# One written order of issue in place of a planner, with fewer spare matmuls, in the first part of a fused attention and Fourier-FFN kernel

## The chip, the cores and the metric

The kernel runs on one core of one Trainium2 chip. The metric is device microseconds of one execution: 995.22 us for the kernel before, the median of 3 runs (994.12 to 995.35).

## The reference, cut to what matters

```python
def _attn_ref(q, k, v, g_norm):            # 8 batches, 8 heads, 576 tokens, head size 64
    kv = np.einsum('bhsd,bhse->bhde', k, v)
    out = np.einsum('bhsd,bhde->bhse', q, kv)
    rms = np.sqrt(np.mean(out * out, axis=-1, keepdims=True) + 1e-06)
    return out / rms * g_norm

def _moe_ref(x, w_ch1, w_ch2):             # x: 8 x 576 x 512; w_ch1: 512 x 2048; w_ch2: 2048 x 512
    X = np.fft.fft(np.fft.fft(x, axis=1), axis=2)
    u = x + np.real(X)
    mu = np.mean(u, axis=-1, keepdims=True)
    var = np.mean((u - mu) ** 2, axis=-1, keepdims=True)
    un = (u - mu) / np.sqrt(var + 1e-06)
    return u + np.maximum(un @ w_ch1, 0.0) @ w_ch2
```

The two weights come as float64 and are decoded on the chip from their bits.

## The kernel before, in words

**What is computed where.** The work has a first part and a late part. The first part takes the eight batches one after the other, with their steps interleaved. For each batch `plan_kv` multiplies keys and values (TensorE, L1197), `plan_q` turns the queries (L1273 for batches 0 and 1, L1279 for the others) and ScalarE copies the turned tile out (`take`, L1283). `plan_out` forms the attention output of three groups of rows t = 0, 1, 2 (L1304); batch 0 has its own form, `plan_first_out` (L1374), with squares (ScalarE L1388), sums (VectorE L1391), a refined reciprocal root (L1403 to L1411) and a scaling (L1419). `plan_fold` folds the rows for the transform: a fold on VectorE (L1501), two sums "even" (L1508, on GpSimd for batch 0), a rounded high part on ScalarE (L1514) and the low remainder (L1517, GpSimd). `plan_seq` is the transform along the tokens (TensorE L1544 for batch 0, L1532 after it; low part on VectorE, L1569), `plan_chn` the one along the channels (L1586; VectorE L1608 and L1628), `plan_turn` the transpose of the result into blocks of 512 tokens (TensorE L1684, high part ScalarE L1693, low part VectorE L1696). Every matmul of weight is done three times, on high and low parts.

As soon as a block of 512 tokens is turned, `plan_early` runs three slices of the FFN on it: `plan_first` (TensorE L1012) and the second product (L1029). Block 0 lies wholly in batch 0. So the first L1012 matmul, step number 1528 below, needs the whole chain of batch 0: keys and values, first output, fold, seq, chn, turn. `plan_w` loads and decodes a weight slice: a load (SyncE, L1729 with the copy at L936), ScalarE L939, VectorE L946 to L956 and L1743, for the first weight a mean on TensorE (L970) and its subtraction (L979), then high (ScalarE L1763) and low (L1768, on GpSimd for the first weight's early slices). The late part, from about 360 us, is the rest of the FFN.

**Spare matmuls.** `plan_spare` (L1075) makes 200 steps of two matmuls that write to a PSUM bank and are read by nobody:

```python
def go(ps=ps):
    for _ in range(0 if pools else 2):
        nc.tensor.matmul(ps.t, still, wide, start=True, stop=True)
```

A step that is issued once the late part's memory is opened (`close`, L2023) emits nothing.

**What sets the order.** Every step is an `Op` with an engine, a cost, a rank, the steps that it needs, and the buffers that it uses, which come from rings of a fixed number of slots (for instance two tiles of queries, six of keys and values, eight PSUM banks). Each engine issues its steps in the order in which they are emitted and waits at the first whose inputs are missing. Before, `Plan.go` (L638) finds that order by playing the steps through with the costs, the ranks and a table `MOVES` of corrections to ranks; it puts spare steps where it has nothing else for TensorE. `Plan.settle` (L796) then applies a table `SHIFTS`: single steps moved on their engine by some places, or left out. `Plan.emit` (L819) emits.

Of the kernel before, what the change touches and what calls it, by code (L numbers as in the profile page):

```python
# [76 lines left out]
SHIFTS = [  # L77
    ("plan_spare.go/PE/-/-", 20, 0),
    ("plan_w.<lambda>/DVE/w1/2", 3, -1),
    ("plan_w.<lambda>/DVE/w1/1", 1, -2),  # L80
    ("plan_q.take/ACT/3/11", 0, 2),
    ("plan_spare.go/PE/-/-", 18, 0),
    ("plan_spare.go/PE/-/-", 26, 0),
    ("plan_w.<lambda>/DVE/w2/2", 1, -4),
    ("plan_first_out.mean/DVE/0/1", 0, -2),
    ("plan_chn.<lambda>/DVE/1/1", 1, -6),
    ("plan_spare.go/PE/-/-", 31, 0),
    ("plan_first_out.square/ACT/0/2", 1, 9),
    ("plan_chn.<lambda>/ACT/1/2", 0, 5),
    ("plan_fold.even.go/DVE/1/1", 1, -2),  # L90
    ("plan_fold.fold/DVE/1/0", 0, -6),
    ("plan_spare.go/PE/-/-", 16, 0),
    ("plan_kv.<lambda>/POOL/2/-", 1, 9),
    ("plan_kv.<lambda>/POOL/5/-", 1, -2),
    ("plan_seq.<lambda>/PE/0/1", 0, -1),
    ("plan_turn.high/ACT/0/0", 0, -2),
    ("plan_out.red/DVE/2/1", 1, 10),
    ("plan_seq.<lambda>/PE/0/0", 1, 2),
    ("plan_q_load.load/SP/1/02", 0, 10),
    ("plan_spare.go/PE/-/-", 9, -4),  # L100
    ("plan_fold.mul/DVE/2/0", 0, -4),
    ("plan_q_load.<lambda>/SP/3/-", 0, 1),
    ("plan_spare.go/PE/-/-", 27, 0),
    ("plan_out.<lambda>/ACT/2/1", 0, -1),
    ("plan_kv.<lambda>/DVE/0/-", 0, 9),
    ("plan_fold.zero/ACT/1/1", 0, 4),
    ("plan_out.<lambda>/ACT/2/1", 1, 1),
    ("plan_first.<lambda>/PE/e0/-", 9, 3),
    ("plan_chn.put.<lambda>/SP/0/0", 1, 2),
    ("plan_kv.<lambda>/SP/1/-", 8, 1),  # L110
    ("plan_fold.zero/ACT/2/2", 0, -1),
    ("plan_chn.mix/DVE/0/0", 1, 5),
    ("plan_y.last/DVE/2/-", 0, -1),
    ("plan_seq.<lambda>/PE/0/0", 0, -2),
    ("plan_out.<lambda>/ACT/1/0", 1, 4),
    ("plan_kv.go/PE/1/-", 1, 1),
    ("plan_w.<lambda>/ACT/w2/0", 0, 9),
    ("plan_first.<lambda>/PE/e0/-", 4, 1),
    ("plan_first_out.mean/DVE/0/2", 0, 1),
    ("plan_first_out.mul/DVE/0/1", 0, 1),  # L120
    ("plan_early.<lambda>/ACT/e0/-", 3, -4),
    ("plan_out.scale/POOL/1/2", 0, 8),
    ("plan_chn.<lambda>/DVE/0/0", 0, 1),
    ("plan_kv.<lambda>/SP/5/-", 8, -2),
    ("plan_q.turn/PE/2/12", 0, 1),
    ("plan_fold.fold/DVE/0/2", 0, -2),
    ("plan_kv.<lambda>/POOL/2/-", 0, 9),
    ("plan_spare.go/PE/-/-", 28, 0),
    ("plan_chn.mix/DVE/1/1", 0, -1),
    ("plan_kv.<lambda>/SP/5/-", 3, 4),  # L130
    ("plan_seq.mm/PE/1/3", 0, -2),
    ("plan_turn.high/ACT/0/0", 1, -2),
    ("plan_out.<lambda>/ACT/2/1", 0, 1),
    ("plan_fold.even.go/POOL/2/0", 1, 3),
    ("plan_fold.low/POOL/1/2", 0, -2),
    ("plan_q.take/ACT/2/11", 0, 7),
    ("plan_early.<lambda>/PE/e0/-", 10, -1),
    ("plan_out.scale/POOL/2/1", 1, 1),
    ("plan_spare.go/PE/-/-", 22, 0),
    ("plan_first_out.red/DVE/0/2", 1, -6),  # L140
    ("plan_fold.zero/ACT/1/2", 0, -2),
    ("plan_q.take/ACT/3/11", 0, -9),
    ("plan_w.<lambda>/DVE/w2/1", 1, 6),
    ("plan_first_out.red/DVE/0/2", 0, 1),
    ("plan_w.<lambda>/DVE/w2/0", 0, 9),
    ("plan_kv.<lambda>/SP/5/-", 7, 7),
    ("plan_w.<lambda>/DVE/w2/1", 0, 8),
    ("plan_first.<lambda>/DVE/e0/-", 1, -1),
    ("plan_spare.go/PE/-/-", 34, 0),
    ("plan_spare.go/PE/-/-", 33, 1),  # L150
    ("plan_chn.<lambda>/ACT/0/1", 0, 3),
    ("plan_q.turn/PE/4/01", 0, 9),
    ("plan_turn.turn/PE/0/1", 0, -2),
    ("plan_q.take/ACT/0/01", 0, -7),
    ("plan_chn.mm/PE/1/0", 1, 4),
    ("plan_turn.high/ACT/0/2", 1, -2),
    ("plan_chn.put.<lambda>/SP/0/0", 1, -2),
    ("plan_q_load.load/SP/1/-", 0, -1),
    ("plan_y.root/ACT/1/-", 0, 3),
    ("plan_w.<lambda>/DVE/w2/1", 5, -6),  # L160
    ("plan_spare.go/PE/-/-", 19, 0),
    ("plan_turn.low/DVE/0/1", 2, -1),
    ("plan_first.<lambda>/PE/e0/-", 0, -2),
    ("plan_turn.high/ACT/4/0", 2, 4),
    ("plan_out.red/DVE/2/1", 1, -3),
    ("plan_kv.<lambda>/POOL/3/-", 0, 1),
    ("plan_kv.<lambda>/ACT/6/-", 0, -2),
    ("plan_q.turn/PE/7/02", 0, 1),
    ("plan_chn.add_r/POOL/5/1", 0, -1),
    ("plan_early.<lambda>/ACT/e1/-", 7, 1),  # L170
    ("plan_y.recip/DVE/4/-", 0, -2),
    ("plan_early.<lambda>/ACT/e2/-", 5, -3),
    ("plan_fold.<lambda>/ACT/2/0", 0, -4),
    ("plan_turn.low/DVE/1/2", 0, 3),
    ("plan_out.red/DVE/6/2", 0, 1),
    ("plan_q.take/ACT/7/10", 0, 1),
    ("plan_first.<lambda>/PE/e2/-", 3, -1),
    ("plan_kv.<lambda>/SP/3/-", 9, -3),
    ("plan_out.mm/PE/3/2", 0, 6),
    ("plan_out.scale/POOL/4/2", 0, -3),  # L180
    ("plan_fold.<lambda>/ACT/3/1", 0, 9),
    ("plan_out.mm/PE/4/0", 0, 1),
    ("plan_chn.<lambda>/DVE/2/2", 1, 2),
    ("plan_chn.<lambda>/DVE/4/0", 0, 4),
    ("plan_first.<lambda>/PE/e3/-", 11, -6),
    ("plan_early.<lambda>/PE/e1/-", 7, -1),
    ("plan_early.<lambda>/ACT/e3/-", 3, -3),
    ("plan_out.og/ACT/6/1", 0, -7),
    ("plan_q.take/ACT/4/11", 0, -10),
    ("plan_turn.turn/PE/1/1", 0, 2),  # L190
    ("plan_seq.mm/PE/3/3", 0, 3),
    ("plan_chn.add_l/POOL/5/1", 0, 1),
    ("plan_seq.low/DVE/3/1", 0, -1),
    ("plan_q_load.load/SP/3/-", 0, 4),
    ("plan_kv.<lambda>/SP/4/-", 4, 2),
    ("plan_early.<lambda>/ACT/e1/-", 3, 1),
    ("plan_chn.<lambda>/DVE/0/0", 1, 9),
    ("plan_seq.mm/PE/3/0", 0, 2),
    ("plan_seq.mm/PE/3/2", 0, 3),
    ("plan_fold.<lambda>/ACT/3/1", 0, 4),  # L200
    ("plan_first.<lambda>/ACT/e3/-", 1, -1),
    ("plan_fold.low/DVE/1/1", 0, -1),
    ("plan_seq.<lambda>/ACT/2/1", 0, -2),
    ("plan_q.take/ACT/2/11", 0, -3),
    ("plan_turn.high/ACT/2/0", 3, 2),
    ("plan_turn.high/ACT/3/0", 3, 1),
    ("plan_chn.add_r/POOL/5/1", 0, -1),
    ("plan_out.<lambda>/ACT/6/0", 0, -2),
    ("plan_fold.<lambda>/ACT/1/1", 0, -4),
    ("plan_fold.low/DVE/2/2", 0, -2),  # L210
    ("plan_turn.low/DVE/1/1", 2, -1),
    ("plan_chn.<lambda>/DVE/3/2", 0, -3),
    ("plan_first.<lambda>/ACT/e2/-", 2, -2),
    ("plan_y.last/DVE/2/-", 0, -3),
    ("plan_kv.<lambda>/POOL/4/-", 1, 3),
    ("plan_seq.mm/PE/5/0", 0, 1),
    ("plan_turn.low/DVE/3/2", 0, -1),
    ("plan_out.og/ACT/5/2", 1, 3),
    ("plan_fold.<lambda>/ACT/1/1", 0, -2),
    ("plan_first.<lambda>/ACT/e2/-", 0, -1),  # L220
    ("plan_chn.mm/PE/5/2", 1, 2),
    ("plan_chn.mm/PE/5/2", 0, -4),
    ("plan_kv.go/PE/5/-", 1, -1),
    ("plan_turn.low/DVE/1/2", 2, -1),
    ("plan_turn.turn/PE/1/0", 1, 1),
    ("plan_chn.<lambda>/DVE/2/1", 0, 4),
    ("plan_fold.even.go/POOL/4/1", 1, -4),
    ("plan_fold.even.go/POOL/2/1", 1, -6),
    ("plan_fold.<lambda>/ACT/3/1", 0, -1),
    ("plan_out.red/DVE/4/1", 0, 6),  # L230
    ("plan_chn.mm/PE/3/0", 1, 9),
    ("plan_kv.<lambda>/POOL/4/-", 1, -2),
    ("plan_first.<lambda>/PE/e2/-", 1, -2),
    ("plan_kv.<lambda>/SP/6/-", 4, 1),
    ("plan_turn.low/DVE/2/0", 2, 9),
    ("plan_q.turn/PE/7/10", 0, 9),
    ("plan_fold.low/POOL/4/1", 0, 1),
    ("plan_fold.low/DVE/4/2", 0, -2),
    ("plan_first.<lambda>/ACT/e1/-", 2, 2),
    ("plan_out.mm/PE/6/2", 0, 2),  # L240
    ("plan_early.<lambda>/ACT/e1/-", 5, 2),
    ("plan_turn.low/DVE/3/1", 1, 2),
    ("plan_chn.put.<lambda>/SP/3/2", 2, 4),
    ("plan_y.mean/POOL/4/-", 0, 2),
    ("plan_first.<lambda>/ACT/e0/-", 0, -3),
    ("plan_chn.<lambda>/ACT/2/1", 0, -1),
    ("plan_turn.high/ACT/0/0", 2, -2),
    ("plan_fold.mul/DVE/3/2", 1, -2),
    ("plan_out.og/ACT/4/2", 1, 1),
    ("plan_seq.low/DVE/5/1", 0, -1),  # L250
    ("plan_kv.<lambda>/POOL/7/-", 1, 1),
    ("plan_turn.high/ACT/4/0", 2, 1),
    ("plan_first.<lambda>/PE/e1/-", 4, -1),
# [2271 lines left out]
```

## Time and profile before

| | |
|---|---|
| median of the runs | 995.22 us (994.12 to 995.35) |
| span of the profiled execution, first to last instruction | 993.5 us |
| TensorE busy | 982.3 us (99%), 6838 matmuls |
| VectorE busy | 690.1 us (69%) |
| ScalarE busy | 363.4 us (37%) |
| GpSimd busy | 397.6 us (40%) |
| DMA | 166.06 MB, mean 167 GB/s |

The page gives the span of the profiled execution and no other time of it; the median of the runs is 1.7 us above it. A busy TensorE is one that has a matmul in flight: matmuls are pipelined, so one of 512 columns shows about 0.39 us, while the next starts about 0.23 us after it. In the windows below, PEclk is the granted clock as a share of 2.4 GHz; 0.5 is 1.2 GHz.

### The profile page before, as it was taken

How to read it: one execution, taken by the hardware profiler on the slowest of the kernel's cores; microseconds unless marked ns; L12 is line 12 of the kernel's file. 1: busy time of each engine (PE TensorE's matmuls, PEld its weight loads, DVE VectorE, ACT ScalarE, POOL GpSimd, SP SyncE). 2: the span in 40 equal slices, each digit the busy share in tenths (PEclk: the TensorE clock that was granted, in tenths of full speed). 3: DMA queues.
4: the chain of work that ended last, by engine and by line, in shares of the span. 5: the costliest groups of instructions: out<-in, count | busy, mean ns of one | idle time of the engine just before them, and what ended most of it. 6: DMA issues, size and time to landing. Idle time of an engine off the chain costs nothing.

```text
span 993.5 us, 17707 instructions
## 1 busy us (share of the span) xinstructions
PE 982.3 (99%) x6838; PEld 858.5 (86%) x6838; DVE 690.1 (69%) x1365; ACT 363.4 (37%) x731; POOL 397.6 (40%) x391
## 2 busy tenths in 40 slices
...
GB/s 231 236 222 271 210 275 230 200 161 165 144 195 117 267 168 192 181 252 211 225 170 159 201 44 212 44 212 53 202 81 187 100 171 115 153 107 149 1 127 43
DMA packets 111240, 166.06 MB, mean 167 GB/s; under 512 B 43710, under 2 KB 71666, under 8 KB 104756
## 3 DMA queue, kind: packets, MB, share of 16 engines
...
q8 instruction: 54, 0.88, 0.4%
...
## 4 chain that ended last, share of the span: by engine, by line
PE 94%; DMA 3%; SPq 1%; DVE 1%; issue 0%; ACT 0%; DVEq 0%; ACTq 0%
PE acc L1029 40%; PE ps_h L1012 20%; PE ps_h L2251 18%; PE ps_f L1586 4%; PE ps_f L1532 3%; PE ps_o L1304 3%; PE ps_k L1197 2%; PE ps_t L1684 2%; DMA vm<-in_v_dram 1%; PE ps_q L1279 1%; DMA draw<-in_dft_s_dram 1%; DMA qt<-in_q_dram 1%; PE ps_s L1084 1%; PE ps_o L1374 0%; SPq L1174 0%
## 5 line engine op out<-in xcount | busy, mean ns | idle before, releaser
L1029 PE MATMUL acc<-w,hh 128*128 128x512 f32 x1150 | 359.3, 394 | 0.0
L1029 PEld LDWEIGHTS acc<-w,hh 128*128 128x128 f32 x1150 | 205.7, 189 | 34.2
L1029 PE MATMUL acc<-w,hl 128*128 128x512 f32 x575 | 224.0, 390 | 0.0
L1021 ACT ACTIVATE hh<-ps_h 128x512 fp32r<-128x512 f32 x144 | 86.2, 598 | 345.8 <-DVE ps_h L2259 170.9
L1012 PE MATMUL ps_h<-unTh,w 128*128 128x512 f32 x576 | 179.3, 392 | 0.0
L1024 DVE SCALAR_TENSOR_TENSOR hl<-ps_h,hh 128x512 fp32r<-128x512 f32 x144 | 98.0, 684 | 92.1 <-ACT hh L1021 91.8
L1029 PEld LDWEIGHTS acc<-w,hl 128*128 128x128 f32 x575 | 108.0, 188 | 23.6
L1012 PEld LDWEIGHTS ps_h<-unTh,w 128*128 128x128 f32 x576 | 106.6, 188 | 21.3
L1012 PE MATMUL ps_h<-unTl,w 128*128 128x512 f32 x288 | 112.3, 390 | 0.0
L2211 POOL TENSOR_TENSOR up<-up 128x512 f32<-128x512 f32 x36 | 46.6, 1295 | 154.4 <-DMA up<-next_scr 119.2
L2259 DVE TENSOR_TENSOR ps_h<-part,ps_h 128x256 f32<-128x256 f32 x144 | 61.1, 425 | 40.9 <-ACT part L2264 23.3
L2259 DVE TENSOR_TENSOR part<-part,ps_h 128x256 f32<-128x256 f32 x108 | 45.4, 420 | 44.4 <-PE ps_h L2251 41.5
L1012 PEld LDWEIGHTS ps_h<-unTl,w 128*128 128x128 f32 x288 | 54.1, 188 | 11.5
L2224 POOL TENSOR_TENSOR uu<-uu,up 128x512 f32<-128x512 f32 x36 | 46.9, 1312 | 36.9 <-ACT up L2216 36.9
L1353 POOL TENSOR_TENSOR x<-x,gb 96x512 f32<-96x512 f32 (+1 forms) x26 | 33.8, 1311 | 45.0 <-ACT x L1320 45.0
L2264 ACT COPY part<-ps_h 128x256 f32<-128x256 f32 x36 | 13.4, 373 | 81.4 <-PE ps_h L2251 81.4
L1696 DVE TENSOR_TENSOR unTl<-ps_t,unTh 128x384 fp32r<-128x384 f32 (+13 forms) x80 | 34.0, 477 | 9.0 <-ACT unTh L1693 8.9
L2358 DVE SCALAR_TENSOR_TENSOR uu<-acc,bz,uu 128x512 f32<-128x512 f32 x35 | 25.0, 750 | 20.2 <-PE acc L1029 20.2
L1508 POOL TENSOR_TENSOR xe<-ab 96x256 f32<-96x256 f32 (+1 forms) x32 | 25.0, 797 | 34.0 <-DVE ab L1501 32.7
L1340 DVE TENSOR_REDUCE ss<-ps_o 96x8 f32<-96x512 f32 (+1 forms) x42 | 27.9, 682 | 14.1 <-ACT ps_o L1336 13.9
L1586 PE MATMUL ps_f<-cd,pt 128*96 128x258 f32 (+1 forms) x288 | 37.0, 283 | 0.0
L1586 PEld LDWEIGHTS ps_f<-cd,pt 128*96 128x96 f32 (+1 forms) x288 | 35.0, 162 | 1.3 <-DVE ss L1340 0.2
(226 smaller groups left out, 1875.9 us busy)
## 6 DMA issues: line engine op xcount, KB each, us to landing
...
```

Of the source, the lines that this page charges most:

```text
L1012: nc.tensor.matmul(ps, w[c][:, kc * P : (kc + 1) * P], unT[a][:, kc, :], start=(kc == 0 and n == 0), stop=(kc == KC - 1 and n == 2),)
L1021: nc.scalar.activation(hh, ps, AF.Relu)
L1024: nc.vector.scalar_tensor_tensor(hl, ps, 0.0, hh.bitcast(F32), ALU.max, ALU.subtract)
L1029: nc.tensor.matmul(acc, hpair[a][:, i * P : (i + 1) * P], w[c], start=(first and n == 0), stop=(last and n == 2),)
L1304: nc.tensor.matmul(pss[s].t[:n, at : at + D], fqs[side].t[half, m, :n], kvt.t[half, m], start=True, stop=True,)
L1353: nc.gpsimd.tensor_tensor(v_, v_, gb[:n].unsqueeze(1).to_broadcast([n, H, D]), ALU.mult)
L1586: nc.tensor.matmul(ps.t[:n, :ND], pt.t[a][:, part, ch, offs[t] : offs[t] + n], cd[:, part, c, ch, :], start=(idx == 0), stop=(idx == 5),)
L1696: nc.vector.tensor_tensor(unTs[j].t[1][:, :, to], view()[:, :, lo:hi], unTs[j].t[0][:, :, to].bitcast(F32), ALU.subtract,)
L2211: lambda p=part: nc.gpsimd.tensor_tensor(p.t[:, 0], p.t[:, 0], p.t[:, 1], ALU.add),
L2224: lambda k=k, ut=ut, p=part: nc.gpsimd.tensor_tensor(ut.t[:, k], ut.t[:, k], p.t[:, 0], ALU.add),
L2251: nc.tensor.matmul(x(to), w.t[:, c, i, kk * P : (kk + 1) * P], rhs(a, kk), start=(kk == 0 and n == 0), stop=(kk == 1 and n == 2),)
L2259: return op("DVE", 415, URGENT, lambda: nc.vector.tensor_tensor(out(), a(), b(), ALU.add), d, bufs)
```

## The change

`SHIFTS`, `MOVES`, `Plan.go`, `Plan.settle` and the planner's constants go. A table `ORDER` has the numbers of 4137 steps in the order of emission; `run` emits it, after testing that no step stands ahead of one that it needs. No step, its work, its engine or its buffers are changed; only places, and the spare steps.

```diff
-SHIFTS = [
-    ("plan_spare.go/PE/-/-", 20, 0),
-    ("plan_w.<lambda>/DVE/w1/2", 3, -1),
...
-MOVES = {
-    "<lambda>/HOST/0/12": 30,
-    "<lambda>/POOL/2": -0.5,
...
+ORDER = """
+5 242 209 381 234 219 210 215 227 226 216 207 206 4 235 42 8 382 383 384 385 386 387 388 213 2 212 218 393 211
+208 222 221 39 389 228 232 237 230 48 23 217 57 214 220 53 239 223 390 391 233 229 392 241 447 238 231 236 394
+240 224 403 452 467 395 396 397 398 0 399 400 225 243 254 401 404 247 245 402 405 406 407 246 408 248 265 244
+256 249 267 269 258 474 454 451 462 466 276 453 277 450 459 460 281 280 449 457 257 250 251 268 259 252 253 270
+261 290 271 260 255 470 266 293 292 482 448 262 263 264 296 272 273 409 410 275 274 294 278 471 298 299 295 461
+468 475 61 472 463 456 415 411 455 464 458 302 279 412 304 305 476 291 469 300 473 282 465 413 306 600 601 414
+301 307 416 283 417 418 419 284 609 287 607 603 606 602 610 604 627 1 612 313 497 477 479 318 319 323 324 314
+325 315 498 501 502 499 480 478 288 285 316 326 503 420 421 500 286 422 327 317 505 481 289 490 308 309 310 320
+483 611 423 311 321 620 613 425 615 616 605 619 491 494 312 322 424 328 329 346 484 487 492 495 485 488 330 348
+493 496 331 486 332 347 362 363 614 628 617 608 364 426 297 629 303 349 489 350 365 427 352 351 366 428 368 367
+334 333 635 504 755 756 338 341 26 357 354 623 625 339 342 344 618 360 624 626 621 371 622 374 358 372 355 506
+429 343 345 430 431 340 432 375 373 356 508 652 376 630 433 379 631 762 763 758 757 760 759 773 761 764 656 657
+377 653 654 434 658 380 361 655 378 643 765 1528 632 1534 1535 1536 1537 1529 1530 1531 507 509 510 511 520 527
...
     def run(self):
...
+        seen = set()
+        line = [self.ops[int(n)] for n in ORDER.split()]
+        for o in line:
+            seen.add(o.n)
+            if any(a.n not in seen for a in o.after):
+                raise RuntimeError(f"{o.key} stands ahead of what it needs")
+        self.emit(line)
```

What stands at some numbers, with the step's place on its own engine in the two orders (counted from 0, spare steps included on TensorE):

| number, step | engine | before | after |
|---|---|---|---|
| 393, load of slice 0 of the second weight | SyncE | 1 | 13 |
| 221 and 222, last keys and values of batch 0 | SyncE | 16, 17 | 17, 16 |
| 239, last turn of queries of batch 0 | TensorE | 14 | 16 |
| 223, last keys-times-values of batch 0 | TensorE | 25 | 17 |
| 394, first step on weight slice 393; 240, copy of 239's result; 224, copy of the keys-times-values | ScalarE | 8, 4, 9 | 7, 8, 9 |
| 243, first output, t = 2 | TensorE | 28 | 18 |
| 470, a turn of queries of batch 1 | TensorE | 38 | 23 |
| 266, first output, t = 0, second product | TensorE | 33 | 24 |
| 302, fold of batch 0, t = 0 | VectorE | 40 | 43 |
| 408, 409, 410, decoding of slice 1 of the first weight | VectorE | 41, 42, 43 | 19, 39, 40 |
| 304 and 305, "even" of batch 0, t = 0 | GpSimd | 15, 16 | 12, 13 |
| 414, low part of slice 1 of the first weight | GpSimd | 14 | 16 |
| 301 and 307, low parts of batch 0, t = 1 and t = 0 | GpSimd | 13, 18 | 17, 18 |
| first and last seq step of batch 0 | TensorE | 46, 62 | 34, 49 |
| 322, seq low part, last of the four | VectorE | 62 | 61 |
| 427 to 430, decoding of slice 2 of the first weight | VectorE | 59, 61, 63, 64 | 74, 78, 81, 84 |
| 328, first chn step of batch 0 | TensorE | 69 | 52 |
| 623, 625, 621, turns of queries of batch 2 | TensorE | 78, 80, 77 | 67, 68, 69 |
| 765, first keys-times-values of batch 3 | TensorE | 89 | 76 |
| 361, the last low part of block 0's turn | VectorE | 97 | 95 |
| 1528, first FFN step of block 0 | TensorE | 93 | 77 |
| 632, a turn of queries of batch 2 | TensorE | 90 | 78 |

Spare steps that emit matmuls: before, 27 on TensorE's places 0 to 8, 13, 19 to 21, 23, 24, 26, 27, 35, 36, 41, 42, 50, 56, 81, 94, 95 and 329; after, 9 on places 1 to 3, 9, 10, 12, 15, 28 and 64.

## Rows read from the trace of the kernel before

**Rows 1.** Windows: stretch, its us, busy us (instructions) by engine, PEclk, DMA, GB/s

```profile
46.70:62.30 15.60, 15.19 (x252) 13.85 (x250) 12.78 (x23) 7.46 (x17) 6.49 (x9) 1.00 0.95 259
62.30:78.80 16.50, 16.41 (x220) 14.63 (x218) 15.62 (x39) 11.99 (x29) 7.22 (x10) 1.00 0.76 201
78.80:360.00 281.20, 281.20 (x2342) 246.83 (x2340) 210.06 (x414) 147.94 (x334) 121.25 (x152) 1.00 0.64 202
360.00:993.50 633.50, 628.54 (x3486) 548.94 (x3484) 422.75 (x835) 178.35 (x316) 252.29 (x201) 1.00 0.41 144
```

**Rows 2.** Windows of the spare matmuls alone: us, PE busy, PEld busy, PEclk, DMA, GB/s

```profile
0.00:9.40 9.40, 7.05 (x18) 5.22 (x18) 1.00 0.73 217
9.40:24.40 15.00, 4.72 (x16) 2.69 (x16) 1.00 1.04 241
34.50:41.30 6.80, 2.07 (x4) 1.16 (x4) 0.52 1.17 202
41.30:78.80 37.50, 3.19 (x10) 1.63 (x10) 1.00 0.87 226
78.80:360.00 281.20, 1.71 (x6) 1.13 (x6) 1.00 0.64 202
```

**Rows 3.** Timeline of TensorE: start, us, instructions merged, idle time before them and its releaser

```profile
9.34 0.88 PE L1273 MATMUL ps_q<-ident,qt 96*64 96x96 f32 x16 [0.59 <-DMA qt<-in_q_dram]
...
13.71 2.20 PE L1273 MATMUL ps_q<-ident,qt 96*64 96x96 f32 x48 [0.26 <-DMA qt<-in_q_dram]
...
24.40 1.57 PE L1374 MATMUL ps_o<-kvt,fq 64*96 64x64 f32 x32
...
33.35 0.81 PE L1374 MATMUL ps_o<-kvg,fq 64*97 64x64 f32 x13 [1.17 <-ACT fq L1283]
...
46.75 0.51 PE L1544 MATMUL ps_f<-cs,xh 96*128 96x290 f32 x2
...
49.69 0.51 PE L1197 MATMUL ps_k<-vm,km 128*64 128x64 f32 x10 [0.20 <-DMA vm<-in_v_dram]
...
78.81 0.73 PE L1012 MATMUL ps_h<-unTh,w 128*128 128x512 f32 x2
...
92.36 0.73 PE L1029 MATMUL acc<-w,hh 128*128 128x512 f32 x2
...
93.85 0.62 PE L1029 MATMUL acc<-w,hh 128*128 128x512 f32 x2
94.31 0.39 PE L1029 MATMUL acc<-w,hl 128*128 128x512 f32 x1
```

**Rows 4.** Timeline of ScalarE, the two loads that it waited for

```profile
24.62 0.64 ACT L939 ACTIVATE ps_a<-raw 128x512 f32<-128x512 f32 x1 [0.86 <-DMA raw<-in_moe_w_ch_dram]
...
32.00 0.93 ACT L1113 ACTIVATE cs<-draw 97x870 fp32r<-97x870 f32 x1 [2.20 <-DMA draw<-in_dft_s_dram]
```

**Rows 5.** Timeline of VectorE, batch 0's chain

```profile
27.23 1.27 DVE L1391 TENSOR_REDUCE ss<-ps_o 96x8 f32<-96x512 f32 x2
...
41.53 0.68 DVE L1501 TENSOR_TENSOR part<-x 97x512 f32<-97x512 f32 x1
...
42.84 1.19 DVE L956 SCALAR_TENSOR_TENSOR wp<-raw,wp 128x512 f32<-128x512 uint32 x1
...
55.49 0.69 DVE L1340 TENSOR_REDUCE ss<-ps_o 96x8 f32<-96x512 f32 x1 [1.94 <-ACT ps_o L1336]
...
59.59 0.45 DVE L1569 TENSOR_TENSOR pt<-ps_f,pt 128x290 fp32r<-128x290 f32 x1
...
71.00 0.69 DVE L1696 TENSOR_TENSOR unTl<-ps_t,unTh 128x384 fp32r<-128x384 f32 x1 [0.84 <-ACT unTh L1693]
```

**Rows 6.** Timeline of GpSimd, the low part of a weight and of batch 0

```profile
48.74 1.27 POOL L1768 TENSOR_TENSOR w<-wa,w 128x512 fp32r<-128x512 f32 x1 [3.24 <-ACT w L1763]
49.98 1.42 POOL L1508 TENSOR_TENSOR part<-part 97x256 f32<-97x256 f32 x2
...
52.20 1.75 POOL L1517 TENSOR_TENSOR xl<-part,xh 97x512 fp32r<-97x512 f32 x1 [0.62 <-ACT xh L1514]
```

More of the change, by code (lines that the diff above doesn't have):

```diff
@@ L76 @@
 }
-SHIFTS = [
-    ("plan_spare.go/PE/-/-", 20, 0),
-    ("plan_w.<lambda>/DVE/w1/2", 3, -1),
[L80 to L253, printed above, removed]
-    ("plan_chn.put.<lambda>/SP/0/2", 2, -4),
-    ("plan_out.<lambda>/ACT/3/2", 1, -4),
-    ("plan_seq.<lambda>/ACT/5/2", 0, -2),
-    ("plan_fold.low/POOL/4/0", 0, -3),
-    ("plan_turn.high/ACT/3/0", 3, 2),
-    ("plan_chn.mix/DVE/0/1", 0, -3),
-    ("plan_out.<lambda>/ACT/3/1", 0, 1),
-    ("plan_out.og/ACT/3/2", 1, 1),
-    ("plan_out.red/DVE/3/1", 1, -9),
-    ("plan_early.<lambda>/PE/e1/-", 5, -1),
-    ("plan_out.mm/PE/4/0", 0, -4),
-    ("plan_spare.go/PE/-/-", 33, 0),
-    ("plan_chn.mm/PE/4/2", 0, 3),
-    ("plan_q.turn/PE/3/12", 0, 4),
-    ("plan_fold.even.go/POOL/4/0", 1, -3),
-    ("plan_seq.<lambda>/ACT/3/1", 0, 1),
-    ("plan_early.<lambda>/PE/e2/-", 10, -2),
-    ("plan_fold.low/DVE/3/1", 0, 1),
-    ("plan_chn.add_l/POOL/1/0", 0, 3),
-    ("plan_first.<lambda>/PE/e3/-", 10, 4),
-    ("plan_turn.low/DVE/1/0", 0, 3),
-    ("plan_q.take/ACT/5/12", 0, -1),
-    ("plan_chn.mix/DVE/4/0", 1, 1),
-    ("plan_early.<lambda>/PE/e3/-", 1, -3),
-    ("plan_out.og/ACT/4/1", 1, 1),
-    ("plan_chn.mix/DVE/5/1", 1, 1),
-    ("plan_seq.<lambda>/ACT/5/3", 0, -2),
-    ("plan_early.<lambda>/PE/e3/-", 3, 3),
-    ("plan_y.root/ACT/6/-", 0, -1),
-    ("plan_w.<lambda>/DVE/w1/2", 5, -6),
-    ("plan_turn.low/DVE/0/1", 0, -6),
-    ("plan_fold.even.go/DVE/5/2", 0, -3),
-    ("plan_first.<lambda>/PE/e0/-", 8, 1),
-    ("plan_turn.low/DVE/1/2", 0, 2),
-    ("plan_fold.mul/DVE/4/1", 0, 4),
-    ("plan_out.scale/POOL/5/2", 0, 9),
-    ("plan_out.<lambda>/ACT/2/2", 0, 2),
-    ("plan_q.take/ACT/2/10", 0, -1),
-]
@@ L566 @@
+ORDER = """
[180 rows of a table added]
+"""
 class Buf:
@@ L588 @@
 class Plan:
-    HOP = 160
-    DRAIN = 120
-    MARGIN = {"PE": 500}
-    AHEAD = 6000
-    LAND = 2200
-    ISSUE = 450
-    SLIP = 100
-    BEGIN = {"PE": 1700, "SP": 300, "ACT": 300, "DVE": 800, "POOL": 800}
-    WARM = 6600
-    COLS = {730: 1536, 880: 1200, 1760: 2560, 440: 576, 1500: 1024, 400: 650, 1200: 1950, 760: 1548, 681: 1536, 460: 1024, 920: 1024}
-    TICK, FULL = 3414, 3400
+    ISSUE = 450
     def __init__(self, rings):
@@ L604, in __init__ @@
         self.ops = []
-        self.now = 0
         self.where = ("-", "-")
@@ L609, in op @@
         o = Op()
-        o.port = port or eng == "POOL"
-        o.wait = wait
         o.eng, o.cost, o.emit, o.lag = eng, cost, emit, lag
```

450 lines of the change are left out of this document (removed), and 167 rows, old and new, of the table ORDER.

## The prediction

> **What bounds the kernel now.** I read the windows first. From 78.8 us to 360 TensorE has a matmul in flight all the time (281.20 of 281.20 us), and in the late part for 628.5 of 633.5 us, at the full clock [rows 1]. Behind 78.8 us the span is TensorE's own work: the end moves by what is taken out of that work, and by how much earlier it can begin. What begins at 78.81 is the first FFN matmul of block 0, step 1528 [rows 3]. Ahead of it TensorE isn't the bound. It starts at 9.34 when queries land, waits again at 13.71 for queries and at 33.35 for a copy [rows 3], and holds spare matmuls: 4.72 us of them from 9.4 to 24.4, 2.07 and 3.19 after that [rows 2]. DMA is at 0.87 to 1.17 of its engines throughout [rows 2]. From 34.5 to 41.3 TensorE's clock is granted at 0.52, the lower of its two levels, 1.2 GHz [rows 2].
>
> So the question is when step 1528 starts. VectorE carries batch 0's chain there: 12.78 of 15.6 us and 15.62 of 16.5 us in the two windows ahead of 78.8 [rows 1].
>
> **The change: what stands ahead of step 1528.** I compared the two orders as sets. Ahead of 1528 TensorE has 69 steps before and 68 after, spare steps left out; the one that goes behind is 632. On VectorE, ahead of the last low part that 1528 needs (361), the sets differ by one sum and two small low parts that go behind and one 0.7 us step that comes ahead: about 0.4 us less. Nothing heavy is pushed past the gate, so a gain there is idle time that goes, not work deferred.
>
> **Spare matmuls.** The table holds nine spare steps. Each emits two matmuls, so 18 of 54 stay and 36 go, not the 45 named. Before, 34 stand ahead of the first output at 24.40 (18 and 16), 14 between 34.5 and 78.8, and 6 behind [rows 2]; after, 14, 4 and 0. The six behind stand among work that never waits, so they come off in full. A 512-column matmul takes the next one's place after 0.62 - 0.39 = 0.23 us [rows 3], 6 x 0.23 = 1.4 us; their busy time, tails counted, is 1.71 [rows 2]. I take -1.4 (bounds -1.7 and -1.4). Those ahead of 24.40 fill waits for data and are worth nothing by themselves. The ten in between that go are part of the next term, since they count only if what they covered is earlier too. Step 632, four matmuls behind the gate instead of ahead, adds 0.3.
>
> **When 1528 starts, step by step.** *Data.* Loads leave SyncE in order. With their sizes from the code (256 KB for two heads of keys or values, 576 for queries, 64 for a rest, 512 for a weight slice), the last keys and values of batch 0 end at 4,514 KB in both orders: 393 moves behind other loads, but stays ahead of these. The trace has 5,026 KB landed at 24.62, 6,455 at 32.00, 10,776 at 49.69 [rows 3, 4], so 193 and then 244 KB/us. The first output can't come earlier. It comes about 0.8 us later: a copy (240) and a weight step (394) now stand directly ahead of 224 on ScalarE. 25.2 instead of 24.40.
>
> *To the fold, 302.* Before, the first sums start at 27.23 and 302, the second fold at 41.53, ends at 42.2 [rows 5]. After, three decoding steps (408 to 410, 3 x 0.7 = 2.1 us) stand ahead of it; some 2 us of waits in that stretch, such as the one behind the late output at 33.35 [rows 3], cover them. I take the 0.8 us through: 43.0. Step 470 is placed ahead of 266 on TensorE and needs 6,820 KB, 32.00 + 365 / 244 = 33.5 us; 266 then ends near 36.5, and its reader on VectorE comes near 40, so 3.5 us cover the wait.
>
> *To the low parts.* Here the old order loses most. GpSimd had 414 ahead of 304 and 305; 414 waited 3.24 us for its input and ran at 48.74, so the two even sums of rows folded at 42.2 ran only from 49.98, and 307 from 52.20 to 53.95 [rows 5, 6]. After, 304 and 305 follow the fold (43.0 + 1.4 = 44.4), then 414, 301 and 307, 1.27 us each: 414 gets its input near 45.1, so 307 ends near 48.9, 5 us earlier. 301 ends at 47.6, some 2 us later than before, because 414 now stands ahead of it. TensorE starts the seq steps at 46.75 before [rows 3]; after, the keys and values ahead of them need 9,143 KB, 32.00 + 2,688 / 244 = 43.0, so near 44.
>
> *To the last seq low part, 322.* Before, 59.59 + 0.45 = 60.0 [rows 5]. After, VectorE has 17 steps from 302 to 322, 11.6 us by their durations, and I allow 1.3 us of wait for slice 1 of the second weight: 43.0 + 12.9 = 55.9. The four steps 427 to 430 went behind (2.8 us), two scalings came ahead (1.4).
>
> *To 361 and 1528.* Between 322 and 361 VectorE then has about 19.5 us of steps, 427 to 432 and the sums among them, and little to wait for: 55.9 + 19.5 + 0.6 = 76.0, and 1528 near 76.2 instead of 78.81: -2.6. TensorE's own work allows it: 46.75 to 78.81 is 32 us for nearly the same steps, less eight spares.
>
> The bounds of this term are on VectorE. Its idle time from 46.7 to 78.8 is 2.8 + 0.9 = 3.7 us [rows 1], two waits of it 1.94 and 0.84 [rows 5]; with every wait gone and 0.4 us of work less, it is -4.1. The other way, the start is 0.8 late and 301 two us late, and if neither is made up, +2.
>
> **Keeping GpSimd and VectorE apart.** One VectorE step took 1.19 us at 42.84 with GpSimd at work, against 0.68 for its like at 41.53 [rows 5]; one GpSimd step 1.75 against 1.27 [rows 6]. So a meeting costs about half a us, and I see two or three ahead of 1528: they're within the 4.1 above, counted with 0.3 in the 0.6 of slack. The Trainium skill, "SBUF — State Buffer", section "Who interferes with whom", says that the engine which comes second is blocked for the whole of the other's instruction. By that a meeting would cost up to 1.27 us here and three meetings 3.8; the rows show less than half, and the sum goes by the rows.
>
> **Finer interleaving.** Behind 1528 the new order changes the kind of step on TensorE more often: runs of one kind go from 147 to 226 up to the last block's FFN. Runs of the two kinds with half-size tiles stay 25. A run that follows turns of queries opens with 0.73 instead of 0.62 [rows 3], 0.11 us; turns of queries go from 17 runs to 30, 13 x 0.11 = 1.4 at most, and I see no such cost for the other kinds. I take +0.6 (bounds 0 and +1.4).
>
> **Sum.** -2.6 - 1.4 + 0.3 + 0.6 = -3.1 us on the span of 993.5, 990.4. The runs stand 1.7 us above the span, so 995.2 - 3.1 = 992.1.
>
> **Rivals.** *Nothing gained at the gate.* VectorE has the same work ahead of 361 and was already 88% busy (28.4 of 32.1 us [rows 1]) there; if one wait replaces another, 1528 stays at 78.8 and only -1.4 + 0.3 + 0.6 = -0.5 is left: 994.7. For it: 301 later, the first output later. Against it: the 5 us of 307.
>
> *More gained.* VectorE waits for nothing from the fold on, and the switches cost nothing: -4.1 - 1.7 + 0.3 = -5.5, 989.7. For it: the waits had plain causes in the order. Against: the late first output.
>
> *Slower: the clock falls for longer.* Before, eight spares and a wait led into one stretch of 6.8 us at 1.2 GHz [rows 2]; the 16 spares from 9.4 to 24.4 ran ahead of it. After, fewer stand there, TensorE waits for 470's queries from about 30 to 33.5, and two spare steps are left to 1528. A stretch of 6.8 us at half speed takes 3.4 us from TensorE; where it falls on seq and chn (44 to 61), which now set the pace, two such stretches cost 6.8: 992.1 + 6.8 = 998.9. It decides from 6.2 us of extra low clock on (3.1 us lost, no gain left), and at 10.2 us the kernel is measurably slower. The Trainium skill, "TensorE: Matmul & The Clock Gate", Part 1, says that the throttled clock is the default and that activity releases it; by that, taking filler out of a stretch with waits is a risk, which the stretch at 34.5 bears out.
>
> *Slower: data.* The new order wants 14,150 KB for steps 621 to 625 (10,264 before), and 15,432 for 765, the last step ahead of 1528. From 10,776 at 49.69, at the 201 GB/s of the last window [rows 1], these land near 67 and 73: in time. Only under 160 KB/us does 765 hold 1528 beyond 78.8; at 140 it is 83, +4.2 instead of -2.6: 998.9.
>
> **How the numbers follow.** Chances: forecast 0.38, nothing at the gate 0.20, more gained 0.20, clock 0.13, data 0.09. Over 0.2% (2 us, about what a measurement can tell here) faster means under 993.2. The forecast's own range, 990.5 to 993.8, lies four fifths below it (0.30), more gained all (0.20), nothing gained a quarter (0.05): 0.55. Slower than 997.2 takes most of the clock and data cases: 0.21. Within: 0.24. The range goes from 987.5 (more gained, and a better start too) to 998.0, where half the slow cases are left out.
>
> **What would show it.** Right: first output near 25, low part 307 near 49, last seq low part near 56, 1528 between 75 and 77.5, no spare behind it, TensorE busy throughout after it. Wrong: 1528 at 78 or later; a low clock of more than 10 us behind 24; a wait for queries or keys on TensorE behind 50 us; or idle TensorE time behind 1528, which the sum has at nothing.

## The result, and the profile after

The kernel after takes 1007.63 us (median of 4 runs, 1006.23 to 1008.31) against 995.29 beside it (994.12 to 997.27): a ratio of 1.0121, 95% interval 1.0108 to 1.0133. It is slower by 1.2%, where 992.1 was forecast, and outside the range. Its profiled execution spans 1004.1 us, 10.6 more than before. A line L1369 of its code is L1869 of the code before, and so on for the body.

In the profiled execution the gate, the start of step 1528, came as forecast, and the loss lies where the sum had nothing. Windows of after (us, busy us and instructions by engine, granted clock, DMA share, GB/s), against [rows 1]:

```profile
62.30:76.50 14.20, 13.98 (x226) 12.26 (x224) 14.17 (x32) 10.34 (x26) 5.31 (x10) 1.00 0.68 170
76.50:200.00 123.50, 123.14 (x1260) 109.31 (x1256) 101.49 (x205) 69.13 (x165) 58.86 (x78) 1.00 0.80 225
200.00:250.00 50.00, 48.91 (x438) 41.93 (x433) 30.49 (x61) 24.88 (x59) 21.07 (x23) 1.00 0.58 188
250.00:340.00 90.00, 89.76 (x559) 76.63 (x558) 70.18 (x131) 43.92 (x100) 40.31 (x45) 1.00 0.43 156
340.00:354.00 14.00, 14.00 (x64) 11.48 (x62) 8.87 (x14) 3.51 (x6) 1.39 (x3) 1.00 0.81 279
354.00:361.00 7.00, 0.29 (x2) 0.00 (x0) 0.00 (x0) 1.05 (x2) 0.00 (x0) 0.82 0.70 254
361.00:370.00 9.00, 8.83 (x30) 7.18 (x31) 4.77 (x7) 2.17 (x5) 1.39 (x3) 0.76 0.14 43
370.00:1004.10 634.10, 629.40 (x3486) 548.87 (x3485) 417.62 (x836) 175.70 (x318) 250.36 (x201) 1.00 0.42 145
```

Two of these stretches in before, which [rows 1] has only within longer ones:

```profile
340.00:354.00 14.00, 14.00 (x65) 11.57 (x64) 10.05 (x16) 5.19 (x10) 1.37 (x3) 1.00 0.33 107
354.00:361.00 7.00, 7.00 (x33) 5.82 (x32) 4.43 (x7) 1.72 (x3) 1.38 (x3) 1.00 0.57 179
```

From 354 to 361 TensorE has next to nothing. DMA was at 0.81 in the stretch ahead, at 0.33 before. The timeline of TensorE in after, its gate (against 78.81 in [rows 3]) and the wait:

```profile
76.56 0.73 PE L512 MATMUL ps_h<-unTh,w 128*128 128x512 f32 x2
...
353.90 0.39 PE L529 MATMUL acc<-w,hl 128*128 128x512 f32 x1
361.17 1.22 PE L512 MATMUL ps_h<-unTh,w 128*128 128x512 f32 x2 [6.88 <-ACT part L1369]
```

The wait is 6.88 us. Then the clock is at 0.76 on the mean of 361 to 370: the next nine 512-column matmuls take 4.00 us, to 365.17, where nine at the full clock take 9 x 0.227 = 2.04 (three start 0.68 us apart from the next three). Together 8.8 us of the 10.6. The chain of waits there (start, us, what):

```profile
343.18 7.47 DMA part_scr<-part
...
350.73 0.60 ACT part L1369
...
351.34 9.11 DMA part_scr<-part
...
360.53 0.59 ACT part L1369
...
361.17 1.65 PE ps_h L512 x3
```

`plan_early` copies each finished tile out of PSUM on ScalarE (L1369) into one of two `part` slots and stores it on ScalarE's queue (L1373). Two stores took 7.47 and 9.11 us, and each next copy waited for a slot; TensorE needs the PSUM bank that the copy empties. The other queue then, SyncE in after:

```profile
341.55 0.38 SPq L436 DMA_DIRECT2D raw<-in_moe_w_ch_dram  x1
341.98 0.50 SPq L1378 DMA_DIRECT2D unT_scr<-unTl  x1
342.58 5.29 SPq L1138 DMA_DIRECT2D u_scr<-x  x4
347.92 2.43 SPq L1378 DMA_DIRECT2D unT_scr<-unTh  x1
350.39 2.86 SPq L1138 DMA_DIRECT2D u_scr<-x  x1
```

Seven stores, which the new order puts behind a weight load that waits for its slot until 341.55. In before SyncE issued such stores from 316.3 to 327.5:

```profile
316.33 5.84 SPq L1638 DMA_DIRECT2D u_scr<-x  x6
...
324.60 1.74 SPq L1878 DMA_DIRECT2D unT_scr<-unTh  x1
326.43 1.04 SPq L1878 DMA_DIRECT2D unT_scr<-unTl  x1
```

ScalarE in after also issues the part stores themselves late: the copy of 323.45 is stored at 343.18, behind other steps of its order:

```profile
323.45 0.59 ACT L1369 COPY part<-acc 128x512 f32<-128x512 f32 x1
...
343.18 0.33 ACTq L1373 DMA_DIRECT2D part_scr<-part  x1
...
355.56 0.59 ACT L1369 COPY part<-acc 128x512 f32<-128x512 f32 x1 [4.25 <-DMA part_scr<-part]
...
360.53 0.59 ACT L1369 COPY part<-acc 128x512 f32<-128x512 f32 x1 [4.38 <-DMA part_scr<-part]
```

### The profile page after: what moved, and what is told of

Read it like the earlier page. It is cut to its first block, busy times and chain, and to the rows that moved or that the text cites. A ratio compares the mean times of both kernels' runs of the same rounds, so it can differ in the third digit from the quotient of the medians.

```text
span 1004.1 us, 17551 instructions
## 1 busy us (share of the span) xinstructions
PE 975.1 (97%) x6802; PEld 849.5 (85%) x6802; DVE 691.2 (69%) x1365; ACT 357.2 (36%) x731; POOL 395.7 (39%) x391
## 4 chain that ended last, share of the span: by engine, by line
PE 89%; DVE 4%; DMA 4%; issue 1%; SPq 1%; ACT 1%; DVEq 0%; ACTq 0%
PE acc L529 37%; PE ps_h L512 19%; PE ps_h L1751 18%; PE ps_f L1032 4%; PE ps_f L1086 3%; PE ps_o L804 2%; PE ps_k L697 2%; DMA part_scr<-part 2%; PE ps_t L1184 1%; DMA qt<-in_q_dram 1%; PE ps_q L779 1%; DMA vm<-in_v_dram 1%; PE ps_q L773 1%; DVE ps_xe L1008 1%; SPq L674 0%
## 5 line engine op out<-in xcount | busy, mean ns | idle before, releaser
L1268 POOL TENSOR_TENSOR w<-wap,w 128x512 fp32r<-128x512 f32 x10 | 13.0, 1296 | 83.2 <-ACT w L1263 83.2
L446 DVE TENSOR_SCALAR ps_a<-ps_a 128x512 f32<-128x512 f32 x32 | 22.2, 694 | 34.0 <-ACT ps_a L439 33.9
L1196 DVE TENSOR_TENSOR unTl<-ps_t,unTh 128x384 fp32r<-128x384 f32 (+18 forms) x80 | 35.1, 472 | 9.0 <-ACT unTh L1193 9.0
L1193 ACT ACTIVATE unTh<-ps_t 128x384 fp32r<-128x384 f32 (+14 forms) x80 | 34.6, 489 | 13.3 <-PE ps_t L1184 11.9
```

The costliest lines, as they stand in the source:

```text
L1196: nc.vector.tensor_tensor(unTs[j].t[1][:, :, to], view()[:, :, lo:hi], unTs[j].t[0][:, :, to].bitcast(F32), ALU.subtract,)
```

## The experiments

All were timed beside the kernel before; ratios are to it, with 95% intervals. An order is given as step numbers of the table; what isn't named stays. The theories: T1, the late stores on SyncE fill DMA when the part stores need it; T2, ScalarE's order; T3, the missing spare matmuls; T4, any order here only moves the wait; T5, meetings of VectorE and GpSimd.

**Where the loss sits.** The orders of before and after have done the same steps, but for two on TensorE, after 1381 and 1361 places (283 us). So they can be joined there.

```diff
-order of after
+order of after, places 1 to 1361, then the steps left, in the order of before   (first kernel)
+order of before, places 1 to 1381, then the steps left, in the order of after   (second kernel)
```

> The order of after for its first 1361 places (TensorE near 283 us; both orders have then done the same steps but for two on TensorE), and from there the order of before. If the loss sits in the late part of the new order (from 300 us on): what after is behind at 283 us, 0.6 us, stays, and no wait at 354: 995.9 (994.5 to 997). If the early part of the new order sows it (T3): 1003 or more.

> The converse: the order of before for its first 1381 places (with its 27 spare steps), the same set of steps, and from there the order of after. If the loss sits in the late part of the new order: the wait at 354 and its low clock come as in after, 9 to 10 us: 1004.5 (1003 to 1006). If it needs the early part too: 997 or less.

Measured: 1.0018 (1.0006 to 1.0030) and 1.0096 (1.0072 to 1.0119). The second shows the wait again, windows:

```profile
340.00:354.00 14.00, 14.00 (x64) 11.47 (x62) 8.85 (x13) 3.50 (x6) 1.38 (x3) 1.00 0.81 283
354.00:361.00 7.00, 0.34 (x3) 0.10 (x1) 0.00 (x0) 1.32 (x3) 0.00 (x0) 0.82 0.70 246
```

The order behind 283 us makes the late wait, 6.66 us here, whatever stands ahead, spares included; the two losses, 0.96% and 0.18%, nearly add up to the 1.21%. The first kernel tells of the rest: its gate is at 78.75, that of before, its late part has no such wait, and yet its span is 997.2, 3.7 more than before. The steps that the two have in common come 2.8 us later than in before at 281 us and 3.7 from 308 on, so most of it is lost between the gate and the seam.

**SyncE's stores first: twelve, then seven.**

```diff
-SyncE: ... 1511 1935 1925 1846 1847 1509 1948 1475 1958 1887 1493 1357 1474 1321 1886 1510 1971
+SyncE: ... 1475 1474 1511 1509 1510 1493 1846 1847 1935 1925 1887 1886 1948 1958 1971   (1321, 1357 further ahead)
+SyncE: ... 1511 1935 1925 1846 1847 1509 1887 1493 1357 1474 1321 1886 1510 1948 1475 1958 1971
```

> The kernel after, with twelve stores on SyncE (eight u_scr stores, the four unT_scr stores of blocks 7 and 8) each put directly behind the step that it needs, so ahead of the weight loads 1935, 1948 and 1958; nothing else moves. Theory T1 (traffic): these stores, held back behind the weight loads, come together from 342 to 354 us, fill the DMA engines, and the part stores of ScalarE then take 7 to 9 us to land instead of about 2; so the 6.9 us of idle TensorE at 354 and the low clock behind it go, 9.1 us come back, 1007.6 - 9.1 = 998.5 (997.5 to 1000), with no TensorE wait over 0.5 us from 300 to 400. Theory T2 (ScalarE's order): a part store is issued up to 19 us behind its copy, behind other steps of ScalarE, and the two part slots come free late whatever the traffic; then quicker landings help in part, a wait of 1 to 3 us and its low clock stay, 1001 to 1004.

> The kernel after, with only the seven SyncE stores that stand behind the weight load 1958 (five u_scr stores, both unT_scr stores of block 8) moved ahead of the weight load 1948, and so behind the load 1935, which the run with twelve moved stores had made late. T1 (traffic): their 4 MB or so move from 342 to 354 into 328 to 341, where no part store is due; the wait at 354 and the low clock behind it go: 998.5 (997.5 to 1000). Rival T4 (the two orders of SyncE and ScalarE only fit together as they stand): a weight slice lands later than ScalarE's place for it, ScalarE holds up the copies behind it, and TensorE waits 3 to 6 us somewhere from 325 to 360: 1002 to 1008.

Twelve: 1.0124 (1.0088 to 1.0161), a miss for both theories. No part copy waits any more, but the weight load behind the stores lands late, ScalarE waits 7.2 us for it with the high part that TensorE needs queued behind, and TensorE waits 4.8 ahead of 341.66. ScalarE's waits from 320 to 350 (us in total, times, longest):

```profile
ACT ps_a L439 <- DMA raw<-in_moe_w_ch_dram: 7.2, 1, 7.2
```

Seven, behind that load: 1.0050 (1.0032 to 1.0068), so some 7 us of the 12 come back, a little less than T1's range has. The same stretches in it:

```profile
340.00:354.00 14.00, 14.00 (x64) 11.61 (x63) 6.90 (x11) 3.92 (x7) 1.38 (x3) 1.00 0.88 293
354.00:361.00 7.00, 5.39 (x23) 3.81 (x22) 6.10 (x10) 2.44 (x5) 0.00 (x0) 1.00 0.52 162
```

1.6 us of idle TensorE are left, in two waits of 0.9 (for a late weight slice) and 0.7 (for a part copy), and the clock doesn't fall. A part store issued at 351.58 frees its slot by 353.63, in 2.05 us:

```profile
351.58 0.33 ACTq L1373 DMA_DIRECT2D part_scr<-part  x1
...
353.63 0.59 ACT L1369 COPY part<-acc 128x512 f32<-128x512 f32 x1 [0.94 <-DMA part_scr<-part]
```

**ScalarE's order.** Each part store of blocks 6 to 8 right behind its copy; first with SyncE's late stores as they are, then with the seven moved.

```diff
-ScalarE: ... 1789 ... 1794 1790 ... 1799 1812 1800 1933 1936 1824 1795 1804 ... 1805 ...
+ScalarE: ... 1789 1790 ... 1794 1795 ... 1799 1800 1812 1933 1936 1824 1804 1805 ...
```

> The kernel after, with each part store of blocks 6 to 8 on ScalarE put directly behind its own copy; SyncE's order stays as it is. T1 (traffic): the stores still meet SyncE's late ones from 342 to 354 and take 7 to 9 us to land; with two slots the third and fourth copy of block 7 still wait; about half of the wait is left: 1002 to 1005, TensorE idle 2 to 5 us near 354. T2 (ScalarE's order): the wait goes, 998.5 (997.5 to 1000).

> The same seven stores moved, and each part store of blocks 6 to 8 on ScalarE directly behind its copy. T1: 998 (997 to 1000), at most 0.5 better than with the seven stores alone. T2 (ScalarE's order has a share of its own): 1 us or more better than with the seven stores alone. T4: 1002 to 1008.

Measured: 1.0085 (1.0056 to 1.0113) and 1.0047 (1.0029 to 1.0065). In the first TensorE's wait goes from 6.88 to 4.8 and one store still takes 8.18 us. So ScalarE's order has some 2.1 us of the wait while the burst is there and nothing that can be told once it is gone; T2 alone falls by this.

**The burst alone, in before.** Seven SyncE stores of before moved behind the weight load 1958.

```diff
-SyncE: ... 1925 1474 1475 1493 1509 1510 1511 1935 1846 1847 1886 1887 1948 1958 1971   (1321, 1357 earlier)
+SyncE: ... 1925 1475 1509 1511 1935 1846 1847 1948 1958 1887 1493 1357 1474 1321 1886 1510 1971
```

> The converse: the kernel before (its own order, written as a table, with all 54 spare matmuls), with only seven SyncE stores (five u_scr stores, the two unT_scr stores of block 8) moved behind the weight load 1958, where the kernel after has them. T1: the part copies from 349 on wait for slots, TensorE goes idle near 354 and its clock falls: 999 to 1004. T2: ScalarE's order is that of before, each part store behind its copy, so nothing: 994.5 to 996.

Measured: 1.0000 (0.9985 to 1.0015). DMA is as full as in after, and two part copies wait for slots (3.43 and 1.06 us), but TensorE has a matmul in flight nearly all the time:

```profile
350.00:355.00 5.00, 5.00 (x24) 4.10 (x23) 4.20 (x7) 2.48 (x5) 0.00 (x0) 1.00 1.01 366
355.00:361.00 6.00, 6.00 (x28) 4.68 (x26) 5.49 (x10) 1.75 (x4) 0.00 (x0) 1.00 0.97 329
```

T1 alone falls by this: the burst is needed for the loss (seven stores moved away end the long wait), but it isn't enough. TensorE loses some 0.5 us here: its steps come 4.5 us later than in before at 334 us, its gate being later too, and 5.0 at 368. In the orders, before runs one slice of block 8 (1848 to 1851) after block 7's last product (1843); after has 1854, another slice, ahead of 1843, and the two slices in turns, so it asks for a PSUM bank sooner: by five steps of three matmuls, 5 x 0.68 = 3.4 us. By this run's own times that would have been a wait of some 3.7 us, an estimate, about half of 6.88. The burst also meets fewer part stores here. It starts at 345.77 and the first part store behind that is issued at 354.33, where after issues three between 343.18 and 351.34, inside its burst (341.98 to 353.25):

```profile
345.77 0.50 SPq L1379 DMA_DIRECT2D unT_scr<-unTl  x1
...
354.33 0.33 ACTq L1374 DMA_DIRECT2D part_scr<-part  x1
...
360.73 0.59 ACT L1370 COPY part<-acc 128x512 f32<-128x512 f32 x1 [3.43 <-DMA part_scr<-part]
```

That the slices in turns and the place of the burst among the part stores are the other half was read, not tried.

**Joins further forward.** The order of after up to step 1528 (350 places) and to 673 places (142 us), then before's; and the first with six stores on SyncE behind the loads.

```diff
-SyncE: ... 767 337 766 335 336 772 353 369 370 780 768 769 910 913 ...   (join at 350)
+SyncE: ... 767 766 772 780 768 769 910 913 337 335 336 353 369 370 ...
```

> The order of after up to step 1528 (350 places of the table), and from there the steps left in the order of before, without before's spares. T1 and T2 alike: the gate at 76.6 (-2.2), the six spares behind it gone (-1.4), step 632 behind it (+0.3), no interleaving to pay: 995.2 - 3.3 = 991.9 (991 to 993), no wait at 354. Rival T3 (fewer spare matmuls or the early order leave a debt that is paid later): 995 or more.

> The order of after for its first 673 places (TensorE near 142 us, where the two orders have done nearly the same set of steps), then the steps left in the order of before, without before's spares. If the gain at the gate is real and only what comes later loses it: after is about 1.6 us ahead there, 995.2 - 1.6 = 993.6 (992.5 to 994.5). If the early order or the missing spares leave a debt (T3): 995.5 or more.

> The order of after up to step 1528 and then that of before, as in the earlier run of this kind, in which TensorE waited 3.65 us for values (vm) at 87.9 and then ran at a low clock; here the six u_scr stores of batch 0 on SyncE stand behind the loads of keys, values and queries that follow them (behind step 913). If these stores made the loads late: the wait and its low clock go, about 5 us, and the gain at the gate stays to the end: 992.2 (991 to 993.5), faster than both kernels. If the loads are late for another reason (DMA is full in any order): 996 to 998.

Measured: 1.0018 (1.0004 to 1.0031), 1.0022 (1.0014 to 1.0031), 1.0026 (1.0011 to 1.0042): three misses. Each has a new wait at its seam: 3.65 us for values at 87.9, 2.4 for queries ahead of 146.65, and 2.7 for a weight's low part ahead of 95.06 in the third, where the values' wait is down to 0.9. They say more of seams than of T3.

**A meeting of VectorE and GpSimd, and spares.** On the kernel joined at 1361: two GpSimd additions behind two sums; then also GpSimd's 301 earlier; four spare steps back; both.

```diff
-GpSimd: ... 1033 1032 1048 1137 1138 ...
+GpSimd: ... 1033 1137 1138 1032 1048 ...
-GpSimd: ... 304 305 600 601 414 301 307 505 481 289 ...
+GpSimd: ... 304 305 301 600 601 414 307 505 481 289 ...
-TensorE: ... 265 244 255 ...
+TensorE: ... 265 spare spare 244 spare spare 255 ...
```

> As the run with the first 1361 places of after and the end of before, with two GpSimd additions of batch 4 (1032 and 1048, x<-x,pm, 2.97 us in after from 206.4) moved behind the even sums 1137 and 1138. In after VectorE's two steps ps_xe<-ab run beside these additions and take 2.64 us, against 0.88 for two such steps at 212.7 with GpSimd idle. If this meeting is what holds ScalarE and VectorE up there (T5): the two steps take about 0.9 us, TensorE's waits at 210.6, 212.3 and one more (0.39, 0.69, 0.4) go, 1.5 us: 994.4 (993 to 995.5). If the waits are ScalarE's order alone: they stay, 995.9.

> As the run with the first 1361 places of after, its two GpSimd additions moved, and the end of before (no difference from before, 0.9999), with one GpSimd step more moved: low part 301 ahead of the two fills 600 and 601, so that the GpSimd steps behind it come about 1.3 us earlier and 505 is done before VectorE reaches step 421 (wp<-raw,wp, 2.51 us at 52.6 there, 0.67 to 0.69 elsewhere). T5 (meetings of GpSimd and VectorE in the new order eat part of the gain at the gate): 421 takes 0.7, VectorE's chain to step 1528 is 1.8 us shorter, 1528 starts 1 to 1.8 us earlier than the 78.1 there: 993.9 (993 to 995). If something else holds 1528 (TensorE's clock, data): it stays near 78, 995.2.

> The same base, with four of the left-out spare steps (8 matmuls) put back on TensorE, two ahead of 244 and two ahead of 255, where it waits for sums of squares near 29 and 31 us. T3 (the spares left out cost clock): the stretch at the lower clock between 34 and 42 us (granted 0.50 there) goes, 1528 starts near 76.6, as in the profiled execution of after that had no such stretch, 1.5 us come back: 993.7 (993 to 995). If those spares are worth nothing, as the prediction had it: 995.2 to 995.7.

> Both edits together: GpSimd's step 301 moved and four spare steps put back. T3 and T5: 992.5 (991.5 to 994), faster than both kernels. If neither counts: 995.2 to 995.7.

Measured: 0.9999 (0.9988 to 1.0011), 1.0003 (0.9989 to 1.0017), 1.0003 (0.9991 to 1.0016), 1.0004 (0.9987 to 1.0021). The first took 1.9 us off its base, though the two intervals overlap a little. VectorE and GpSimd in the base, then VectorE in the run:

```profile
209.26 2.63 DVE L1008 TENSOR_TENSOR ps_xe<-ab 97x256 f32<-97x256 f32 x2
...
208.64 2.97 POOL L1119 TENSOR_TENSOR x<-x,pm 96x514 f32<-96x514 f32 x2
```

```profile
208.64 0.90 DVE L1008 TENSOR_TENSOR ps_xe<-ab 97x256 f32<-97x256 f32 x2
```

The two VectorE steps go from 2.63 to 0.90 us, and two TensorE waits of 0.4 and 0.7 behind them are gone. In the other three the time stayed, and all three expectations of a gain are misses. The gates were at 75.60, 77.24 and 74.26 against 78.12 in their base; 77.24 is within what one order shows from execution to execution (below). With both edits the profiled span is 992.4, 1.1 under before, from a gate 4.6 earlier: the rest is lost again behind it, part of it in waits of 0.2 to 1.2 us.

**The spares by themselves.** The kernel before with 18 of its 54 spare matmuls, the first ones.

```diff
-27 spare steps
+9 spare steps (the first nine)
```

> The kernel before, its order written as a table, with only the first 9 of its 27 spare steps (18 of 54 spare matmuls); the order of all else is that of before. By the prediction's term: the six behind 78.8 come off, -1.4, those that filled waits count nothing: 993.8 (993 to 995.3). Rival T3 (the spares keep TensorE's clock up): more low clock between 10 and 60 us than the 6.8 us of before, and 2 to 5 us lost: 997 to 1000.

Measured: 1.0005 (0.9991 to 1.0019), between the two. From 20 to 41.3 us the clock is at 0.50:

```profile
20.00:41.30 21.30, 19.41 (x246) 18.73 (x244) 12.39 (x28) 9.28 (x19) 4.41 (x6) 0.50 1.01 231
```

The gate comes at 82.11, 3.3 later, and the six behind the gate give a part back. How much of the 3.3 is the clock's isn't shown: with all spares the order of before had its gate at 82.23 in one execution of three (the run with the burst alone).

**Everything mended.** The three edits with joins at 1168 and 1241 places, and the order of after to its end with all edits, the seven stores and the part stores included.

> All three edits (the GpSimd additions moved, step 301 moved, four spare steps put back) on the order of after for its first 1168 places (TensorE near 245 us), then the order of before. In the run with the cut at 1361 the lead over before, 5.3 us at 88, was 3.5 at 250 and 0.9 at 306. If the places from 1168 to 1361 of the new order give the 2.6 us back: the lead stays near 3.3, 995.3 - 3.3 = 992 (991 to 993.5), faster than both. If any change of order at a seam costs as much: 994.5 to 996.

> The same with the cut at 1241 (TensorE near 262 us): if the loss from 250 to 306 lies behind 262 in the new order, as with the cut at 1168, 992 (991 to 993.5); else 994.5 to 996.

> The kernel after with its whole own order and all edits: the seven SyncE stores ahead of 1948, each part store of blocks 6 to 8 behind its copy, the GpSimd additions moved, step 301 moved, four spare steps put back. The run with the first two alone was at 1.0047 of before. If the meetings and spares count as in the joined kernels (2 to 4 us of lead at 250) and only the late part's own leftover waits (0.9 and 0.8 near 350, 1.4 later) stay: 997 (995.5 to 998.5). If the late part takes what the early part gains: 1000.

Measured: 1.0026 (1.0016 to 1.0037), 1.0011 (1.0003 to 1.0020), 1.0022 (1.0009 to 1.0035). The first two are misses: their seams cost a wait of 3.1 and one of 1.4 and the clock behind it. The third shows that the edits take the new order from 1.0121 to 1.0022. No version beat before.

## Why the prediction was wrong

**The gate was right in the profile.** First output at 25.34 (near 25), first seq at 45.57 (near 44), step 1528 at 76.56 (76.2). The low part 307 ended at 50.49 (48.9), and the last seq low part, 322, at 58.17, where 55.9 was worked out:

```profile
57.36 0.81 DVE L1069 TENSOR_TENSOR pt<-ps_f,pt 128x290 fp32r<-128x290 f32 x2
```

So the chain was up to 2.3 us late, and the stretch from 322 to 1528 took 18.4 us instead of 20.3: that the end fits to 0.4 is luck. This was also the best execution of its kind: in nine later kernels with the same order up to there, 1528 started at 76.87 to 78.84, and the median of the ten is 78.0; with before's order and spares it was 78.17, 78.81 and 82.23. The -2.6 is nearer to -0.8, and five of the ten lie at 78 or later, which the prediction had named as a sign of being wrong. The runs of after that weren't profiled took 1.3 to 2.1 us more than the profiled one, at a mean clock of 0.991 against 0.996, which fits.

**The meetings were sized too low.** I took half a us for one. In after VectorE's step at 51.04 came while GpSimd ran, and ended behind GpSimd's next step too:

```profile
51.04 2.53 DVE L456 SCALAR_TENSOR_TENSOR wp<-raw,wp 128x512 f32<-128x512 uint32 x1
...
50.44 1.30 POOL L853 TENSOR_TENSOR x<-x,gb 96x512 f32<-96x512 f32 x1
51.67 0.13 POOL L789 MEMSET fq<- 128x4 f32 x1
51.73 1.30 POOL L620 TENSOR_TENSOR cd<-draw,cd 128x516 fp32r<-128x516 f32 x1
```

With 505 out of the way, in the run with 301 moved, it took 0.69: the meeting cost 1.84. The half us that the prediction took reads as what was left of GpSimd's work, not as the price of any meeting. In before the step at 42.84 [rows 5] ended at 44.03, 0.54 behind GpSimd's:

```profile
41.69 1.80 POOL L1508 TENSOR_TENSOR xe<-ab 96x256 f32<-96x256 f32 x2 [2.74 <-DVE ab L1501]
```

In after the step ended at 53.57, again 0.54 behind GpSimd's end. The Trainium skill's rule ("SBUF — State Buffer", "Who interferes with whom"), that the second is blocked for the whole of the other's instruction, would have given up to 1.27; here the trace agrees with its kind, and goes beyond its size. The order doesn't keep the two apart: VectorE's sums ps_xe<-ab of 96 rows take 797 ns on the mean behind the gate, 652 before.

**The spares.** 18 stay and none stands behind the gate, as worked out. That those ahead were worth nothing by themselves doesn't hold for the clock: left out of before, it was at 0.50 from 20 to 41.3; put back into the new order, it rose from 0.50 to 1.00 between 34.5 and 41.3. In the time it showed neither way. The rival with the clock named the stretch, but not the size: after itself had no low clock there. Ahead of seq and chn half the low stretch is also too high a price: the run with 18 spares in before has 21.3 us of it where before has 6.8, some 7 us by that price, and took 0.5 us more (at most 1.9), with 1.4 us of spares less behind the gate.

**The failed step** is the one that ends the first part: behind 78.8 "the span is TensorE's own work", and "idle TensorE time behind 1528, which the sum has at nothing". I compared the two orders as sets up to 1528 and carried before's busy TensorE over to the rest, though SyncE's and ScalarE's order was new there too. What the runs showed in its place is the wait of 6.88 us at 354 and the low clock behind it, made by the order behind 283 us. By the profile: -2.3 at the gate, -1.1 for spares and step 632, +8.8 at 354, +1.7 of other waits (0.36 to 200 us, 1.09 to 250, 0.24 to 340) leave 3.5 of the 10.6. That has no wait in the profile. A part of it belongs to the term for finer interleaving (+0.6, at most 1.4), which was mis-sized. Up to the last block's FFN, the FFN falls into 77 runs instead of 53 on TensorE, and 32 of them instead of 10 open behind a turn of the result (ps_t), counted in the two timelines; behind turns of queries it is 13 instead of 10. The first matmul of such a run holds up the next for 0.32 us instead of 0.23, in before as in after, where the prediction saw such a cost behind turns of queries alone:

```profile
295.44 0.49 PE L1184 MATMUL ps_t<-ident,x 96*128 96x96 f32 x4
295.71 0.71 PE L529 MATMUL acc<-w,hh 128*128 128x512 f32 x2
...
296.49 0.62 PE L529 MATMUL acc<-w,hh 128*128 128x512 f32 x2
```

By the start times all openings of FFN runs take 1.8 us more than in before. No run tried this by itself, and the cause of the other 1.7 stays open.
